# Summing squares over the chunks of d_model on VectorE before the product over partitions, and a norm issued in three parts

## The chip, the cores and the metric

The kernel runs on one core of one Trainium2 chip. The metric is device time in microseconds, the median of three runs. Five engines share the work: TensorE (PE, with its weight loads as PEld), VectorE (DVE), ScalarE (ACT), GpSimd (POOL) and SyncE (SP). Each works through its own instructions in the order in which they were issued, and waits on semaphores for the others.

## What is computed

Retention attention on 8 sequences of 576 tokens, 8 heads of 64, then a SwiGLU feed-forward network (FFN) with an RMS norm in front of it, all in float32 (the weights come as float64 and are rounded on the chip):

```python
scores = scale * np.matmul(q, k.transpose(0, 1, 3, 2))
ret = scores * Dmat                       # decay, zero above the diagonal
x = np.matmul(ret, v)                     # -> (4608 tokens, 512)
rms = np.sqrt(np.mean(x * x, axis=-1, keepdims=True) + 1e-06)
xn = x / rms * rms_g
g = xn @ w_gate                           # (512, 1536)
out = (g / (1 + np.exp(-g)) * (xn @ w_val)) @ w_out
```

## The kernel before

x is kept transposed: d_model lies on the partitions in four chunks of 128 (a chunk is a pair of heads), the tokens lie along the free axis. The FFN works on units of 384 tokens, so there are 12 units, and four of them fit on the chip.

**Attention.** One step (`attention_step`) is one key tile of 128 and one block of queries for a pair of heads: `scores` (two products `s`, L145, and their decay multiply on VectorE, `ret`, L149), then `finish`, which runs `values` (two products `av`, L165) of the step before. After the last key tile ScalarE copies `av` into the unit's `x` (L173). At the third and fifth step of a job the next job's q and k are turned on TensorE (`tp_q`, `tp_k`, L115) and copied by ScalarE (L118). Three buffers hold `s`, two are shared by `tp` and `av`.

**Norm.** When the last chunk of a unit is written, `values` returns true and `finish` calls `norm_1`: ScalarE squares the whole unit (`sq`, L185, 1536 columns), TensorE sums the squares over d_model with the squares as the weights and one column of 1/512 as the moving operand (`ms`, L188: 3 token tiles by 4 chunks, 12 products), VectorE adds epsilon (`r`, L193), GpSimd raises to -1/2 (L194), VectorE lays the result on the diagonals of three square tiles (`diag`, L197). One step later `norm_2` spreads it over the partitions with one product (`rb`, L206), and VectorE scales x by it in four instructions (L210).

**FFN.** A unit has 24 projections (`gate` and `val` in turn, L218, 4 products of 384 columns each), SiLU on ScalarE (L228) and a multiply on VectorE (`h`, L233), then 9 contract steps of 4 products of 512 columns (`out`, L241). Three PSUM buffers are shared by `gate`, `val`, `out`, `ms` and `rb`.

A product of float32 operands is two matmul instructions and two weight loads in the profile, so that the 12 products `ms` of a norm are 24 there.

**Order.** One loop (L386 to L406) issues either an attention step or an FFN step. An FFN step is taken when the FFN is behind a fixed share of the attention (`due`) and a unit is ready, else an attention step; where the next unit isn't ready, attention goes on alone. `turned` runs `norm_2` and makes the unit ready. Each pass also counts as a step for the norm: `norm_2` comes at the second pass after `norm_1`. Every second attention step rounds one chunk of the weights, six instructions on VectorE and one on ScalarE (L323 to L354), until all 36 are done.

Of the kernel before, what the change touches and what calls it, by code (L numbers as in the profile page):

```python
# [10 lines left out]
F32 = mybir.dt.float32  # L11
U32 = mybir.dt.uint32
AF = mybir.ActivationFunctionType
ALU = mybir.AluOpType
P = 128


def _decay_table(H, S, D):
    """T[p, h, c] = gamma_h ** (c - p) / sqrt(D) where c >= p, else 0: a key tile that begins at
    token t uses column q - t for query q."""  # L20
    gamma = 1.0 - 2.0 ** (-5.0 - np.arange(H, dtype=np.float64))
    rel = np.arange(S)[None, :] - np.arange(P)[:, None]
    t = np.where(rel >= 0, gamma[:, None, None] ** np.maximum(rel, 0)[None], 0.0) / np.sqrt(D)
    return np.ascontiguousarray(t.transpose(1, 0, 2)).astype(np.float32)
# [3 lines left out]
def kernel(  # L28
# [11 lines left out]
    nc = tc.nc  # L40
    B, H, S, D = q.shape
    NTOK, DM = out.shape
    DFF = moe_w_gate.shape[1]
    NHP = H // 2  # head pairs, which are also the 128-row chunks of d_model
    NF = DFF // P
    NKT = -(-S // P)  # key tiles; the last one is short
    JT = 6  # token tiles of a loaded q or k
    PT = S // JT
    U = 384  # tokens of a unit of the FFN
    NU = NTOK // U  # L50
    XBUFS = 4  # units of x on chip
    EPS = 1e-6
    assert (D, DM, NHP * P) == (64, H * D, DM) and S % JT == 0 and NTOK % U == 0

# [9 lines left out]
    ps_f = ctx.enter_context(tc.tile_pool(name="ps_f", bufs=3, space=PS))  # L64

    ident = const.tile([P, P], F32, name="ident")
    mean_w = const.tile([P, 1], F32, name="mean_w")
# [10 lines left out]
    st = [{} for _ in jobs]  # L78
    x_of = {}

# [1 line left out]

    def load(j):
        b, hp = jobs[j]
# [19 lines left out]
        st[j]["v"] = t  # L104

    def turn(j, nm):
        """q or k of a head pair with (head, d) on the partitions."""
        d = st[j]
        t = att.tile([P, S], F32, tag=nm + "T", name=f"{nm}T_{j}")
        tv = t.rearrange("p (j t) -> p j t", j=JT)  # L110
        half = JT // 2
        for n in range(2):
            tp = ps_m.tile([P, half, PT], F32, tag="m", name=f"tp_{nm}_{j}_{n}")
            for i in range(half):
                nc.tensor.transpose(  # L115
                    out=tp[:, i], in_=d[nm + "raw"][:, n * half + i], identity=ident[:PT, :PT]
                )
            nc.scalar.copy(out=tv[:, n * half : (n + 1) * half], in_=tp)  # L118
        d[nm + "T"] = t

    def blocks(b):
        """The queries of a sequence, cut where the FFN's units are."""
        cuts = [0] + [c - b * S for c in range(0, NTOK, U) if 0 < c - b * S < S] + [S]
        return list(zip(cuts[:-1], cuts[1:]))

# [6 lines left out]
        ]  # L132

    def scores(j, q0, q1, kt):
        """ret[key, query] of one key tile and one block of queries, for both heads."""
        d = st[j]
        hp = jobs[j][1]
        k0, k1 = kt * P, min(kt * P + P, S)
        lo, n = max(q0, k0), k1 - k0
        w = q1 - lo  # L140
        ret = att.tile([P, 2, U], F32, tag="ret", name=f"ret_{j}_{q0}_{kt}", bufs=3)
        ss = [ps_s.tile([P, 512], F32, tag="s", name=f"s_{j}_{q0}_{kt}_{e}") for e in range(2)]
        for e in range(2):
            r = slice(e * D, e * D + D)
            nc.tensor.matmul(  # L145
                ss[e][:n, :w], lhsT=d["kT"][r, k0:k1], rhs=d["qT"][r, lo:q1], start=True, stop=True
            )
        for e in range(2):
            nc.vector.tensor_tensor(  # L149
                out=ret[:n, e, :w], in0=ss[e][:n, :w],  # L150
                in1=decay[:n, 2 * hp + e, lo - k0 : q1 - k0], op=ALU.mult,
            )
        d["ret", q0, kt] = ret
# [19 lines left out]
            nc.scalar.copy(out=x_of[u][:, hp, c0 : c0 + q1 - q0], in_=av[:, : q1 - q0])  # L173
        return last and hp == NHP - 1 and (b * S + q1) % U == 0

# [1 line left out]

    NS = U // P

    def norm_1(u):  # L180
        """1 / rms with the tokens on the partitions, as the diagonals of square tiles."""
        x = x_of[u]
        ms = ps_f.tile([P, 512], F32, tag="f", name=f"ms_{u}")
        sq = ffn.tile([P, NHP, U], F32, tag="sq", name=f"sq_{u}", bufs=1)
        nc.scalar.activation(out=sq, in_=x, func=AF.Square)  # L185
        for s in range(NS):
            for c in range(NHP):
                nc.tensor.matmul(  # L188
                    ms[:, s : s + 1], lhsT=sq[:, c, s * P : s * P + P], rhs=mean_w,
                    start=(c == 0), stop=(c == NHP - 1),  # L190
                )
        r = ffn.tile([P, NS], F32, tag="r", name=f"r_{u}")
        nc.vector.tensor_scalar(out=r, in0=ms[:, :NS], scalar1=EPS, scalar2=None, op0=ALU.add)  # L193
        nc.gpsimd.tensor_tensor(out=r, in0=r, in1=mhalf.to_broadcast([P, NS]), op=ALU.pow)  # L194
        diag = ffn.tile([P, NS, P], F32, tag="diag", name=f"diag_{u}", bufs=1)
        for s in range(NS):
            nc.vector.tensor_scalar(  # L197
                out=diag[:, s], in0=ident, scalar1=r[:, s : s + 1], scalar2=None, op0=ALU.mult
            )
        return diag  # L200

    def norm_2(u, diag):
        """The diagonals summed over the partitions are 1 / rms in a row, on every partition."""
        x = x_of[u]
        rb = ps_f.tile([P, 512], F32, tag="f", name=f"rb_{u}")
        nc.tensor.matmul(  # L206
            rb[:, :U], lhsT=ones, rhs=diag.rearrange("p s t -> p (s t)"), start=True, stop=True
        )
        for c in range(NHP):
            nc.vector.scalar_tensor_tensor(  # L210
                out=x[:, c], in0=x[:, c], scalar=rms_g[:, c : c + 1], in1=rb[:, :U],
                op0=ALU.mult, op1=ALU.mult,
            )
# [34 lines left out]
            nc.sync.dma_start(out=out[u * U + s * P : u * U + s * P + P, :], in_=o)  # L248

    def ffn_steps(u):  # L250
        """(columns of the tensor engine, what to do)"""
        hs, ps = {}, {}
        for f in range(NF):
            yield NHP * U, lambda f=f: gate(u, f, hs)
            yield NHP * U, lambda f=f: value(u, f, hs)
        for s in range(U // P):
            for f0 in range(0, NF, 4):
                yield 4 * DM, lambda s=s, f0=f0: contract(u, s, f0, f0 + 4, hs, ps)

# [1 line left out]

    LAG = 0.17
    ready = []
    behind = []
    turning = []

    def upto(t):
        """The last unit that attention writes to, in the step of t or the one behind it."""
        j, q0 = t[:2]
        return (jobs[j][0] * S + q0) // U  # L270

    def finish():
        if behind and values(*behind.pop()):
            turning.append(norm_1(len(ready) + len(turning)))

    def turned():
        if turning:
            norm_2(len(ready), turning.pop(0))
            ready.append(len(ready))

    def attention_step(n, t):
        j = t[0]
# [8 lines left out]
                if j + 3 < len(jobs):  # L291
                    load(j + 3)

# [1 line left out]

    def columns(w, src, f):
        cut = slice(f * P, f * P + P)
# [2 lines left out]
    def rows(f):  # L300
        return w_out[:, f], lambda x: x, moe_w_out, slice(None), slice(f * P, f * P + P)

    chunks = [
        c
        for f in range(NF)
        for c in (columns(w_gate, moe_w_gate, f), columns(w_val, moe_w_val, f))
    ] + [rows(f) for f in range(NF)]
# [13 lines left out]
        raw_chunks[i] = view  # L321

    def round_chunk(i):  # L323
        """float64, as pairs of words, to the nearest float32. The mantissa is summed as
        (1.m * 2 ** 20), in one rounding; sign and exponent are put together as bits, with
        the exponent held in float32's range."""
        if i not in raw_chunks:
            return
        dst = chunks[i][0]
# [34 lines left out]
    with tc.manual_schedule():  # L364
# [17 lines left out]
        attn = [(n, t) for j in range(len(jobs)) for n, t in enumerate(tiles(j))]  # L382
        n_attn = len(attn)
        ffn_cols = sum(c for u in range(NU) for c, _ in ffn_steps(u))
        did_a, did_f, unit, steps, waited = 0, 0, 0, None, False
        while did_a < n_attn or unit < NU:  # L386
            if turning and waited:
                turned()
            waited = bool(turning)
            if steps is None and unit < len(ready):  # L390
                steps = ffn_steps(unit)
            due = did_a == n_attn or (did_a / n_attn - LAG) * ffn_cols > did_f * (1 - LAG)
            if steps is not None and (due or unit + XBUFS <= upto(attn[did_a][1])):
                got = next(steps, None)
                if got is None:
                    unit, steps = unit + 1, None
                    continue
                did_f += got[0]
                got[1]()
            elif did_a < n_attn:  # L400
                attention_step(*attn[did_a])
                did_a += 1
                if did_a > 8 and did_a % 2:
                    weights_to(n_chunks + 1)
                if did_a == n_attn:
                    finish()  # L406
# [27 lines left out]
```

## Time and profile before

| what | value |
|---|---|
| median of 3 runs | 1737.68 us (1737.16 to 1738.85) |
| span of the profiled execution | 1732.1 us |
| mean granted clock of TensorE | 0.917 |
| TensorE busy | 1609.2 us, 93% |
| VectorE busy | 387.0 us, 22% |
| ScalarE busy | 213.7 us, 12% |
| GpSimd busy | 10.9 us, 1% |

The profiled execution's own time is its span, from the first instruction to the last; the median of the runs lies 5.6 us above it, which is what lies around the instructions. A granted clock of 1.00 is 2.4 GHz and 0.50 is 1.2 GHz. Busy time of a pipelined engine doesn't say that it works at its peak, so the wait lists and the granted clock are read beside it.

### The profile page before, as it was taken

To read this page: it belongs to the slowest core of one execution; us is meant where nothing else is said; L and a number is where in the kernel's file an instruction comes from. 1 tells how busy PE (TensorE), PEld (TensorE's weight loads), DVE (VectorE), ACT (ScalarE), POOL (GpSimd) and SP (SyncE) were. 2 spreads that over 40 slices of the span, in tenths; PEclk is the share of its full clock that TensorE was granted. 3 is DMA by queue.
4 is the path that set the end of the run, shared out by engine and by line. 5 is a ranking of instruction groups with operands and counts; after the bars stand their busy time and mean duration, and the time that the engine had idled before them with its cause. 6 is when DMAs were issued, how large, how long until landed. Compare 5 with 4: busy or idle time off the path is not lost.

```text
span 1732.1 us, 14109 instructions
## 1 busy us (share of the span) xinstructions
PE 1609.2 (93%) x5784; PEld 842.0 (49%) x5784; DVE 387.0 (22%) x940; ACT 213.7 (12%) x422; POOL 10.9 (1%) x18
## 2 busy tenths in 40 slices
PE   5778976999999999999999899999999899999899
PEld 2334532554454554554554554454554554455454
DVE  2655375121111111211111211310111310410110
ACT  1112121110011110110110100110110100200000
POOL 0000000000000000000000000000000000000000
PEclk9556976999998999998999899899899899989899
DMA  6333232100100100100000101200101200100000
GB/s 180 100 88 89 60 113 80 27 14 13 33 14 20 31 17 20 47 0 20 26 21 19 41 1 28 59 0 13 27 7 32 56 1 0 46 1 6 12 0 18
DMA packets 134927, 59.89 MB, mean 35 GB/s; under 512 B 115920, under 2 KB 128208, under 8 KB 134864
## 3 DMA queue, kind: packets, MB, share of 16 engines
q1 hardware_dynamic: 119360, 37.77, 8.7%
q10 hardware_dynamic: 15504, 21.24, 3.9%
q8 instruction: 45, 0.74, 0.2%
q14 instruction: 18, 0.15, 0.0%
HBM read 49.55 MB, written 9.44 MB: 34 GB/s over the span
## 4 chain that ended last, share of the span: by engine, by line
PE 88%; DVE 6%; ACT 4%; issue 1%; DMA 1%; POOLq 0%; SPq 0%; ACTq 0%; DVEq 0%
PE gate L218 23%; PE out L241 22%; PE val L218 22%; PE s L145 8%; PE av L165 7%; PE ms L188 3%; PE tp_k L115 2%; PE tp_q L115 1%; ACT exp L338 1%; DVE exp L342 1%; ACT sq L185 1%; ACT kT L118 1%; PE rb L206 1%; DVE exp L339 1%; ACT x L173 1%
## 5 line engine op out<-in xcount | busy, mean ns | idle before, releaser
L241 PE MATMUL out<-w_out,h 128*128 128x512 f32 x864 | 402.8, 619 | 23.4 <-DVE w_out L352 23.4
L218 PE MATMUL gate<-x,w_gate 128*128 128x384 f32 x1152 | 411.9, 502 | 5.8 <-DVE x L210 5.8
L218 PE MATMUL val<-x,w_val 128*128 128x384 f32 x1152 | 397.8, 488 | 0.0
L218 PEld LDWEIGHTS gate<-x,w_gate 128*128 128x128 f32 x1152 | 221.7, 195 | 168.3 <-issue 15.9
L218 PEld LDWEIGHTS val<-x,w_val 128*128 128x128 f32 x1152 | 216.6, 190 | 151.4 <-issue 5.8
L241 PEld LDWEIGHTS out<-w_out,h 128*128 128x128 f32 x864 | 165.3, 197 | 232.6 <-issue 191.2
L149 DVE TENSOR_TENSOR ret<-s,decay 128x384 f32<-128x384 f32 (+4 forms) x480 | 160.2, 374 | 527.3 <-PE s L145 526.0
L233 DVE TENSOR_TENSOR h<-silu,val 128x384 f32<-128x384 f32 x144 | 79.8, 554 | 612.4 <-PE val L218 612.1
L145 PE MATMUL s<-qT,kT 64*128 64x384 f32 (+4 forms) x960 | 189.9, 433 | 23.5 <-DVE ret L149 23.3
L145 PEld LDWEIGHTS s<-qT,kT 64*128 64x128 f32 (+1 forms) x960 | 88.2, 198 | 146.9 <-issue 109.5
L228 ACT ACTIVATE silu<-gate 128x384 f32<-128x384 f32 x144 | 70.7, 491 | 697.7 <-PE gate L218 686.7
L165 PE MATMUL av<-ret,v 128*64 128x384 f32 (+4 forms) x960 | 156.2, 407 | 0.0
L165 PEld LDWEIGHTS av<-ret,v 128*64 128x64 f32 (+1 forms) x960 | 51.3, 146 | 74.9 <-issue 61.1
L188 PE MATMUL ms<-mean_w,sq 128*128 128x1 f32 x288 | 55.5, 325 | 26.9 <-ACT sq L185 26.9
L188 PEld LDWEIGHTS ms<-mean_w,sq 128*128 128x128 f32 x288 | 54.4, 293 | 29.1 <-ACT sq L185 29.1
L247 ACT COPY o<-out 128x512 f32<-128x512 f32 x36 | 21.1, 586 | 341.7 <-PE out L241 341.7
L115 PE MATMUL tp_k<-ident,kraw 96*128 96x96 f32 x192 | 33.5, 291 | 19.4 <-ACT kT L118 15.5
L115 PE MATMUL tp_q<-ident,qraw 96*128 96x96 f32 x192 | 32.6, 291 | 18.3 <-DMA qraw<-in_q_dram 9.7
L173 ACT COPY x<-av 128x384 f32<-128x384 f32 (+1 forms) x64 | 25.5, 399 | 177.4 <-PE av L165 153.4
L118 ACT COPY kT<-tp_k 128x288 f32<-128x288 f32 x64 | 25.5, 399 | 129.0 <-PE tp_k L115 128.9
L115 PEld LDWEIGHTS tp_k<-ident,kraw 96*128 96x128 f32 x192 | 20.5, 156 | 41.4 <-ACT kT L118 21.9
L115 PEld LDWEIGHTS tp_q<-ident,qraw 96*128 96x128 f32 x192 | 21.1, 160 | 32.1 <-issue 15.7
(33 smaller groups left out, 261.4 us busy)
## 6 DMA issues: line engine op xcount, KB each, us to landing
qraw<-in_q_dram SPq DMA_DIRECT2D x64, 144.0 KB, 2.5
kraw<-in_k_dram SPq DMA_DIRECT2D x64, 144.0 KB, 2.5
out_dram<-o SPq DMA_DIRECT2D x36, 256.0 KB, 2.1
v<-in_v_dram SPq DMA_DIRECT2D x64, 128.0 KB, 2.5
w<-in_moe_w_gate_dram ACTq DMA_DIRECT2D x12, 512.0 KB, 3.4
w<-in_moe_w_val_dram ACTq DMA_DIRECT2D x12, 512.0 KB, 3.6
w<-in_moe_w_out_dram ACTq DMA_DIRECT2D x12, 512.0 KB, 3.4
decay<-decay_table ACTq DMA_DIRECT2D x4, 576.0 KB, 6.3
```

Of the source, the lines that this page charges most:

```text
L115: nc.tensor.transpose(out=tp[:, i], in_=d[nm + "raw"][:, n * half + i], identity=ident[:PT, :PT])
L118: nc.scalar.copy(out=tv[:, n * half : (n + 1) * half], in_=tp)
L145: nc.tensor.matmul(ss[e][:n, :w], lhsT=d["kT"][r, k0:k1], rhs=d["qT"][r, lo:q1], start=True, stop=True)
L149: nc.vector.tensor_tensor(out=ret[:n, e, :w], in0=ss[e][:n, :w], in1=decay[:n, 2 * hp + e, lo - k0 : q1 - k0], op=ALU.mult,)
L165: nc.tensor.matmul(av[e * D : e * D + D, lo - q0 : q1 - q0], lhsT=d["v"][:n, e, kt], rhs=ret[:n, e, : q1 - lo], start=(kt == 0), stop=last,)
L173: nc.scalar.copy(out=x_of[u][:, hp, c0 : c0 + q1 - q0], in_=av[:, : q1 - q0])
L188: nc.tensor.matmul(ms[:, s : s + 1], lhsT=sq[:, c, s * P : s * P + P], rhs=mean_w, start=(c == 0), stop=(c == NHP - 1),)
L218: nc.tensor.matmul(ps[:, :U], lhsT=w[:, c, f * P : f * P + P], rhs=x_of[u][:, c], start=(c == 0), stop=(c == NHP - 1),)
L228: nc.scalar.activation(out=hs[f], in_=ps[:, :U], func=AF.Silu)
L233: nc.vector.tensor_tensor(out=h, in0=hs[f], in1=ps[:, :U], op=ALU.mult)
L241: nc.tensor.matmul(ps[s][:, :DM], lhsT=hs[f][:, s * P : s * P + P], rhs=w_out[:, f], start=(f == 0), stop=(f == NF - 1),)
L247: nc.scalar.copy(out=o, in_=ps[s][:, :DM])
```

## The change

`norm_1` is cut in two. The new `norm_0`, called where `norm_1` was, squares the unit on ScalarE and then adds the four chunks on VectorE, in place, in two instructions: 768 columns, then 384. `norm_1` sums what is left over the partitions, with one product a token tile (3 instead of 12), and the rest of it is as it was. `turned` is now called at every pass and counts: the third pass after `norm_0` issues `norm_1`, the third after that issues `norm_2` and makes the unit ready. Only the oldest of the units in `turning` is counted. Comments and docstrings are removed, which moves the line numbers.

```diff
-    def norm_1(u):
+    def norm_0(u):
         x = x_of[u]
-        ms = ps_f.tile([P, 512], F32, tag="f", name=f"ms_{u}")
         sq = ffn.tile([P, NHP, U], F32, tag="sq", name=f"sq_{u}", bufs=1)
         nc.scalar.activation(out=sq, in_=x, func=AF.Square)
+        n = NHP
+        while n > 1:
+            n //= 2
+            nc.vector.tensor_tensor(
+                out=sq[:, :n], in0=sq[:, :n], in1=sq[:, n : 2 * n], op=ALU.add
+            )
+        return sq
+
+    def norm_1(u, sq):
+
+        ms = ps_f.tile([P, 512], F32, tag="f", name=f"ms_{u}")
         for s in range(NS):
-            for c in range(NHP):
-                nc.tensor.matmul(
-                    ms[:, s : s + 1], lhsT=sq[:, c, s * P : s * P + P], rhs=mean_w,
-                    start=(c == 0), stop=(c == NHP - 1),
-                )
+            nc.tensor.matmul(
+                ms[:, s : s + 1], lhsT=sq[:, 0, s * P : s * P + P], rhs=mean_w,
+                start=True, stop=True,
+            )
...
     def finish():
         if behind and values(*behind.pop()):
-            turning.append(norm_1(len(ready) + len(turning)))
+            u = len(ready) + len(turning)
+            turning.append([u, 0, norm_0(u), 0])
 
     def turned():
-        if turning:
-            norm_2(len(ready), turning.pop(0))
-            ready.append(len(ready))
+
+
+        if not turning:
+            return
+        t = turning[0]
+        t[3] += 1
+        if t[3] < 3:
+            return
+        u, part, got, _ = t
+        if part == 0:
+            turning[0] = [u, 1, norm_1(u, got), 0]
+        else:
+            norm_2(u, got)
+            turning.pop(0)
+            ready.append(u)
...
-            if turning and waited:
-                turned()
-            waited = bool(turning)
+            turned()
```

On TensorE, at the norm of the seventh unit (number 6, counted from 0), the order before is this; `av_0` writes the unit's last chunk, `s_384` and `av_384` belong to the next attention steps, `tp_k` turns k:

```order
L165 MATMUL av_0_3985<-ret_0_2_3988,v_3511 64x128 x2
L188 MATMUL ms_4018<-mean_w,sq_4019 128x1 x12
L145 MATMUL s_384_1_0_4041<-qT_3873,kT_3920 128x192
L145 MATMUL s_384_1_1_4042<-qT_3873,kT_3920 128x192
L165 MATMUL av_384_4047<-ret_384_0_4008,v_3511 64x192 x2
L115 MATMUL tp_k_0_4051<-ident,kraw_3736 128x96 x3
L115 MATMUL tp_k_1_4056<-ident,kraw_3736 128x96 x3
L206 MATMUL rb_4071<-diag_4036,ones 128x384
L218 MATMUL gate_0_4077<-x_3468,w_gate 128x384 x4
```

The same place on TensorE after the change, from the same `av_0` on:

```order
L165 MATMUL av_0_3943<-ret_0_2_3946,v_3469 64x128 x2
L145 MATMUL s_384_1_0_3981<-qT_3831,kT_3878 128x192
L145 MATMUL s_384_1_1_3982<-qT_3831,kT_3878 128x192
L165 MATMUL av_384_3987<-ret_384_0_3966,v_3469 64x192 x2
L115 MATMUL tp_k_0_3991<-ident,kraw_3694 128x96 x3
L115 MATMUL tp_k_1_3996<-ident,kraw_3694 128x96 x3
L145 MATMUL s_384_2_0_4012<-qT_3831,kT_3878 128x192
L145 MATMUL s_384_2_1_4013<-qT_3831,kT_3878 128x192
L165 MATMUL av_384_3987<-ret_384_1_3980,v_3469 64x192 x2
L197 MATMUL ms_4020<-mean_w,sq_3976 128x1 x3
L145 MATMUL s_384_3_0_4032<-qT_3831,kT_3878 128x192
L145 MATMUL s_384_3_1_4033<-qT_3831,kT_3878 128x192
```

Two attention steps now stand between `av_0` and `ms`, and three more stand between `ms` and `rb`, which is followed by `gate_0` as before. The other norms are of three kinds: numbers 0, 4, 6, 7, 9 and 10 have two attention steps between, as here; 1 and 3 have one contract step and one attention step; 2, 5, 8 and 11 have projections alone.

On VectorE, the same place before; `ret` is the decay multiply of the attention steps:

```order
L149 TENSOR_TENSOR ret_384_0_4008<-s_384_0_0_4009,decay 128x192
L149 TENSOR_TENSOR ret_384_0_4008<-s_384_0_1_4010,decay 128x192
L193 TENSOR_SCALAR r_4033<-ms_4018 128x3
L197 TENSOR_SCALAR diag_4036<-ident,r_4033 128x128 x3
L149 TENSOR_TENSOR ret_384_1_4040<-s_384_1_0_4041,decay 128x192
L149 TENSOR_TENSOR ret_384_1_4040<-s_384_1_1_4042,decay 128x192
L210 SCALAR_TENSOR_TENSOR x_3468<-x_3468,rms_g,rb_4071 128x384 x4
```

And on VectorE after the change, where the two additions to `sq` are new:

```order
L149 TENSOR_TENSOR ret_384_0_3966<-s_384_0_0_3967,decay 128x192
L149 TENSOR_TENSOR ret_384_0_3966<-s_384_0_1_3968,decay 128x192
L188 TENSOR_TENSOR sq_3976<-sq_3976 128x768
L188 TENSOR_TENSOR sq_3976<-sq_3976 128x384
L149 TENSOR_TENSOR ret_384_1_3980<-s_384_1_0_3981,decay 128x192
L149 TENSOR_TENSOR ret_384_1_3980<-s_384_1_1_3982,decay 128x192
L149 TENSOR_TENSOR ret_384_2_4011<-s_384_2_0_4012,decay 128x192
L149 TENSOR_TENSOR ret_384_2_4011<-s_384_2_1_4013,decay 128x192
L202 TENSOR_SCALAR r_4024<-ms_4020 128x3
L206 TENSOR_SCALAR diag_4027<-ident,r_4024 128x128 x3
L149 TENSOR_TENSOR ret_384_3_4031<-s_384_3_0_4032,decay 128x192
```

The additions stand ahead of the `ret` of the next attention step, and `r` and `diag` ahead of the `ret` of the step that follows `ms`.

At the end of the program, on TensorE, the last norm (number 11) stood alone before: the last `av`, then `ms`, `rb` and `gate_0`:

```order
L165 MATMUL av_192_6220<-ret_192_4_6463,v_5960 64x64 x2
L188 MATMUL ms_6475<-mean_w,sq_6476 128x1 x12
L206 MATMUL rb_6497<-diag_6493,ones 128x384
L218 MATMUL gate_0_6503<-x_5991,w_gate 128x384 x4
L218 MATMUL val_0_6510<-x_5991,w_val 128x384 x4
```

After the change the FFN of unit 10 (`x_5244`) begins behind the last `av`, and the norm of unit 11 stands within it:

```order
L165 MATMUL av_192_6132<-ret_192_4_6164,v_5890 64x64 x2
L215 MATMUL rb_6180<-diag_6151,ones 128x384
L227 MATMUL gate_0_6186<-x_5244,w_gate 128x384 x4
L227 MATMUL val_0_6193<-x_5244,w_val 128x384 x4
L227 MATMUL gate_1_6200<-x_5244,w_gate 128x384 x4
L197 MATMUL ms_6207<-mean_w,sq_6176 128x1 x3
L227 MATMUL val_1_6218<-x_5244,w_val 128x384 x4
L227 MATMUL gate_2_6225<-x_5244,w_gate 128x384 x4
L227 MATMUL val_2_6232<-x_5244,w_val 128x384 x4
L215 MATMUL rb_6239<-diag_6214,ones 128x384
```

Both FFNs that are left at the end of attention now run one behind the other.

## Rows read from the trace of the kernel before

**Rows 1.** Page, part 1: busy time of each engine, share, instructions

```profile
PE 1609.2 (93%) x5784; PEld 842.0 (49%) x5784; DVE 387.0 (22%) x940; ACT 213.7 (12%) x422; POOL 10.9 (1%) x18
```

**Rows 2.** Waits of TensorE from 290 us on: total us, times, longest us

```profile
PE ms L188 <- ACT sq L185: 22.6, 11, 2.1
...
PE gate L218 <- DVE x L210: 5.8, 7, 1.1
PE rb L206 <- DVE diag L197: 2.0, 1, 2.0
```

**Rows 3.** Groups by line, `ms`: busy us, mean ns | idle before

```profile
L188 PE MATMUL ms<-mean_w,sq 128*128 128x1 f32 x288 | 55.5, 325 | 26.9 <-ACT sq L185 26.9
```

**Rows 4.** Chain that ended last, in order of time: start us, us, what

```profile
103.59 5.28 PE ms L188 x24
...
302.93 2.84 PE ms L188 x24
...
326.32 2.58 PE val L218 x8
```

**Rows 5.** Behind `ms`, units 1 to 11: length, PE, PEld, DVE, ACT, POOL, PEclk, DMA

```profile
305.77:309.60 3.83, 3.83 (x11) 1.98 (x11) 0.84 (x4) 0.80 (x2) 0.85 (x1) 0.55 0.02 4
348.17:354.40 6.23, 6.23 (x12) 3.42 (x12) 0.84 (x4) 0.49 (x1) 0.85 (x1) 0.55 0.00 0
553.33:558.60 5.27, 5.27 (x7) 2.17 (x8) 0.84 (x4) 0.00 (x0) 0.85 (x1) 0.51 0.00 0
713.53:719.00 5.47, 5.47 (x16) 2.06 (x16) 1.86 (x6) 0.80 (x2) 0.85 (x1) 0.50 0.24 54
806.19:811.20 5.01, 5.01 (x7) 2.03 (x7) 0.84 (x4) 0.00 (x0) 0.85 (x1) 0.51 0.00 0
970.99:982.10 11.11, 9.84 (x26) 5.13 (x26) 3.56 (x10) 0.80 (x2) 0.85 (x1) 0.51 0.12 27
1117.51:1122.00 4.49, 4.49 (x15) 1.93 (x16) 1.86 (x6) 0.80 (x2) 0.85 (x1) 0.53 0.00 0
1229.75:1234.70 4.95, 4.21 (x11) 1.23 (x10) 2.14 (x8) 0.00 (x0) 0.85 (x1) 0.53 0.00 0
1373.77:1385.00 11.23, 9.96 (x25) 5.14 (x26) 3.56 (x10) 0.90 (x3) 0.85 (x1) 0.52 0.12 26
1519.11:1528.00 8.89, 7.76 (x16) 3.06 (x16) 3.96 (x10) 0.00 (x0) 0.85 (x1) 0.50 0.00 1
1629.20:1637.30 8.10, 5.38 (x8) 2.65 (x9) 3.03 (x8) 0.00 (x0) 0.85 (x1) 0.51 0.01 2
sum 74.58, PE 67.46 PEld 30.81 DVE 23.33 ACT 4.58 POOL 9.36; mean PE 6.13 PEld 2.80 DVE 2.12 ACT 0.42 POOL 0.85
```

**Rows 6.** Groups by line, VectorE: shapes, count | busy us, mean ns

```profile
L339 DVE TENSOR_SCALAR exp<-exp 128x512 uint32<-128x512 f32 x36 | 15.4, 428 | 47.4 <-ACT exp L338 47.4
...
L342 DVE SCALAR_TENSOR_TENSOR exp<-w,exp 128x512 uint32<-128x512 uint32 x36 | 24.9, 692 | 1.2
...
L233 DVE TENSOR_TENSOR h<-silu,val 128x384 f32<-128x384 f32 x144 | 79.8, 554 | 612.4 <-PE val L218 612.1 <-ACT silu L228 0.3
```

**Rows 7.** Timeline at the norm of unit 6: start us, us, engine, instruction

```profile
963.67 0.48 ACT L173 COPY x<-av 128x384 f32<-128x384 f32 x1 [0.53 <-PE av L165]
964.18 1.48 ACT L185 ACTIVATE sq<-x 128x1536 f32<-128x1536 f32 x1
...
971.03 0.16 DVE L193 TENSOR_SCALAR r<-ms 128x3 f32<-128x3 f32 x1 [7.15 <-PE ms L188]
...
972.22 0.68 DVE L197 TENSOR_SCALAR diag<-ident,r 128x128 f32<-128x128 f32 x3 [1.03 <-POOL r L194]
...
972.81 0.62 DVE L149 TENSOR_TENSOR ret<-s,decay 128x192 f32<-128x192 f32 x2
```

**Rows 8.** Timeline at the first norm: TensorE behind VectorE's queue

```profile
119.00 1.01 PE L145 MATMUL s<-qT,kT 64*128 64x192 f32 x2 [2.41 <-DVE ret L149]
```

**Rows 9.** A stretch of attention alone, columns as in rows 5

```profile
940.00:962.00 22.00, 20.91 (x100) 9.67 (x100) 5.10 (x16) 3.10 (x8) 0.00 (x0) 1.00 0.24 64
```

More of the change, by code (lines that the diff above doesn't have):

```diff
@@ L384 @@
         ffn_cols = sum(c for u in range(NU) for c, _ in ffn_steps(u))
-        did_a, did_f, unit, steps, waited = 0, 0, 0, None, False
+        did_a, did_f, unit, steps = 0, 0, 0, None
         while did_a < n_attn or unit < NU:
-            if turning and waited:
-                turned()
-            waited = bool(turning)
+            turned()
             if steps is None and unit < len(ready):
```

## The prediction

> **What bounds the kernel now.** I read the busy shares first. TensorE is busy 93% of the span and VectorE 22% [rows 1], so only what shortens TensorE's own queue or its waits can pay. The wait list of TensorE came next: from 290 us on, behind the rounding of the weights, it waits for anything but transposes at three places, and all three belong to the norm. It waits 22.6 us in 11 norms for the squares, 5.8 us for the first scaled chunk of x and 2.0 us for the diagonals [rows 2]. The groups by line then show the norm's products: 288 instructions with one moving column, busy 55.5 us [rows 3]. The chain in order of time shows a norm's 24 in 2.84 us at full clock and in 5.28 us at half [rows 4]. Last comes the granted clock behind the products, and this is what a busy share hides. In each of the 11 stretches that begin where `ms` ends, the clock stands between 0.50 and 0.55 for 3.8 to 11.2 us [rows 5]. I found no low clock elsewhere after 290 us, and a stretch of attention alone runs at 1.00 with TensorE busy 20.91 of 22 us [rows 9]. So TensorE stands still or loads one-column products for some 7 us, its clock falls, and the attention and FFN work behind it pays too.
>
> **What is removed, units 1 to 11.** Four terms, each from rows:
>
> - The products. 55.5 us less the 5.28 us of the first norm leaves 50.2 us. A quarter of the instructions remains: 6 of 24, which at full clock is 2.84 / 4 = 0.71 us a norm, 7.8 us in all. Gain 42.4 us.
> - The wait for the squares, 22.6 us, goes: two steps stand ahead of `ms` now. What is late in its place is priced below.
> - The low clock. At half clock, busy work takes twice its time, so a stretch of length L at mean clock c loses (1 - c) L. Over the eleven rows that is 1.72 + 2.80 + 2.58 + 2.73 + 2.45 + 5.44 + 2.11 + 2.33 + 5.39 + 4.45 + 3.97 = 36.0 us. Idle time in them, 74.58 - 67.46 = 7.1 us, isn't lengthened by the clock, which takes off half of it, 3.6 us [rows 5]. 32.4 us are left.
> - The last norm. Its wait for the diagonals, 2.0 us, has nothing behind it to fill it before; afterwards the FFN of unit 10 does. Of the seven waits for x, 5.8 us, five stay, where `gate_0` follows `rb` directly: 5 x 0.8 = 3.9 us. Gain 2.0 + 1.9 = 3.9 us.
>
> Together 101.3 us.
>
> **The first norm.** It lies among the rounding of the weights, at half clock: 5.28 us of products [rows 4] behind 1.48 us of squares (the length of unit 6's, rows 7). Afterwards 6 instructions at half clock take 1.32 us, and the additions enter VectorE's queue, on which the rounding runs. If squares and additions stay in the chain the gain is 6.76 - 1.32 - 1.48 - 1.56 = 2.4 us; if both are hidden, 5.4 us; if VectorE's extra waits in a full queue eat it, 0. I take 2.4.
>
> **What is added.** The two additions read 768 and 384 columns, 1152 in all, from two operands on the chip. No such instruction stands in the trace. By columns, the nearest are 428 ns and 692 ns for 512, and 554 ns for 384 with an operand in PSUM [rows 6]: 0.84, 1.35 and 1.44 ns a column, so between 0.96 and 1.66 us a norm. An added instruction can't take less than nothing, so there is no gain side. I take the middle one, which has two tensor operands on the chip too: 1.56 us. VectorE has room for 12 x 1.56 = 19 us; the price is the order, not the time.
>
> The additions wait for the squares, and the `ret` of the next attention step is queued behind them; `s` needs its buffer back from `ret`, and `av` needs `ret` itself. Such a queue is seen to stop TensorE: at the first norm a product `s` waited 2.41 us for a `ret` that stood behind other work of VectorE [rows 8]. Counted from the end of the unit's last `av`: copy and squares until 2.0 us (963.67 to 965.66), additions until 3.6, the first `ret` until 3.9 [rows 7]. TensorE has two attention steps and their transposes meanwhile, some 3 us that don't need that `ret`, but `tp_k` also needs a copy by ScalarE that is queued behind the squares. I put the stop at 1.2 to 1.5 us. Behind `ms`, `r` to the end of `diag` holds VectorE's queue for 972.22 + 0.68 - 971.03 = 1.9 us [rows 7], and the `ret` of the step issued after `ms` stands behind that; TensorE has about 1 us of other work there, so it stops for another 1 us. Before, the same `diag` was hidden because one attention step's `ret` was already through. Together 2.5 us at each of the five norms between two attention steps (4, 6, 7, 9, 10): 12.5 us. Ends: 0, where the steps cover all, and 5 us a norm, 25 us. At the six other norms an FFN step, 2.58 us or longer [rows 4], stands between, needs nothing of VectorE, and covers the additions: nothing.
>
> **The clock after the change** is the cost that no row shows. At the six norms inside the FFN, TensorE no longer stands still and the products take 0.71 us; I expect 1.00 throughout. At the five others TensorE stops twice, for 1 to 1.5 us each, with the six one-column instructions between. What fell before had about 2 us of waiting and then `ms`; so one end is no fall, 0 us, and the other a fall at all five, as long as now: 2.73 + 5.44 + 2.11 + 5.39 + 4.45 = 20.1 us [rows 5]. I take three falls at the mean of 4.0 us: 12 us.
>
> The Trainium skill speaks against the change here: "TensorE: Matmul & The Clock Gate", section "A second HAM failure mode: psum-queue depth-cycling", describes a kernel whose TensorE stood idle briefly and often between groups of matmuls, so that its clock went up and down between the two levels. The rows before the change agree in part: attention alone with short gaps stays at 1.00 [rows 9], and the clock falls where a longer wait meets `ms` [rows 5]. By that rule more of the norms fall than I take; it is the second rival below.
>
> **The sum.** 101.3 + 2.4 - 12.5 - 12 = 79.2 us less. The profiled span of 1732.1 us becomes 1652.9; with the 5.6 us by which the median of the runs lies above the span, 1658.5. I say 1658 us.
>
> **Rivals.**
>
> First, the clock stays up everywhere. For it: attention alone at 1.00 [rows 9]. Against it: the stops above. 79.2 + 12 = 91.2 us less, 1646 us.
>
> Second, the clock still falls behind every norm, because any short stop around one-column products is enough, not only 2 us of waiting and 24 of them. The price is what it costs now, 32.4 us, and the remaining products at half clock, 11 x 0.71 = 7.8 us more, in place of 12: 28.2 us more, 1687 us. For it: it fell in 11 of 11 norms. Against it: three quarters of the products and, at six norms, the whole wait are gone.
>
> Third, slower than before: VectorE's queue stops TensorE for its whole chain at every one of the 12 norms, FFN steps between or not, and each stop brings a low clock as long as that of unit 6. The chain is 3.9 + 1.9 = 5.8 us [rows 7], 69 us in all instead of 12.5; the clock costs 5.44 + 0.71 = 6.2 us, 68 us in 11 norms instead of 12. That is 112 us more, 1771 us. It decides from (101.3 + 2.4) / 12 = 8.6 us of new loss a norm. Against it: `gate`, `val` and `out` wait for nothing that VectorE is late with, and only half of the norms stand between attention steps.
>
> Fourth, the additions do not come off the path because `ms` itself waits for them as it waited for the squares. With two attention steps ahead, some 4 us, against 3.6 us of copy, squares and additions, this is a few tenths at five norms and is within the range.
>
> **How the numbers follow.** Forecast (two to four falls) 0.50; no fall 0.30; a fall at every norm 0.15; slower 0.02; the rest, 0.03, is a loss between the second and the third that I can't name. The likeliest case with the ends of its stops and of the additions runs from 1648 to 1671. The range that leaves out 2 in 10 takes in the first rival with stops smaller than assumed and stops short at the second: 1638 to 1686. A measurement of this kernel can tell about 0.2%, 3.5 us. Faster by more than that 0.97, within it 0.01, slower 0.02.
>
> **What would show it.** Right: 72 `ms` instructions, some 8 to 10 us busy; no wait of `ms` for ScalarE; granted clock 1.00 through norms 1, 2, 3, 5, 8 and 11; new waits of `s` or `av` for `ret` at norms 4, 6, 7, 9 and 10, 1 to 1.5 us each; additions of about 1.0 and 0.5 us; the last norm inside the FFN of unit 10 with TensorE busy. Wrong: low clock at norms inside the FFN, waits for `ret` of 3 us or more, or a wait of `ms` for the additions as long as the one for the squares was.

## The result: 4% faster, and the profile after

The changed kernel takes 1669.5 us (median of 4 runs, 1667.4 to 1675.7) against 1738.3 us, also of 4; the ratio is 0.9602, 95% interval 0.9579 to 0.9625. 1658 us were forecast, in a range of 1638 to 1686. The profiled execution spans 1665.9 us, 66.2 us less than before.

Busy shares and granted clock on the page after, as in [rows 1]:

```profile
span 1665.9 us, 13657 instructions
...
PE 1558.4 (94%) x5568; PEld 798.7 (48%) x5568; DVE 404.0 (24%) x964; ACT 212.8 (13%) x422; POOL 10.9 (1%) x18
```

TensorE is busy 50.8 us less, with 216 matmuls fewer; VectorE is busy 17 us more. The groups by line, which answer to [rows 3], show the products and the additions:

```profile
L188 DVE TENSOR_TENSOR sq<-sq 128x768 f32<-128x768 f32 (+1 forms) x24 | 18.2, 758 | 18.8 <-ACT sq L184 18.4
...
L197 PE MATMUL ms<-mean_w,sq 128*128 128x1 f32 x72 | 11.8, 279 | 0.0
```

72 products are left and nothing is waited for in front of them. TensorE's waits from 290 us on, as in [rows 2] (total us, times, longest):

```profile
PE gate L227 <- DVE x L219: 10.8, 6, 3.4
...
PE s L145 <- DVE ret L149: 4.2, 7, 1.2
PE av L165 <- ACT qT L118: 1.0, 2, 0.5
```

The wait for the squares and the one for the diagonals are gone. The wait of `gate` for the scaled x has grown from 5.8 to 10.8 us, and `s` now waits for `ret`.

The granted clock around norms 1, 3, 4, 5, 6, 7, 8, 9, 10 and 11, in this order (length, busy times, and the clock in the third column from the right):

```profile
298.00:311.00 13.00, 12.03 (x46) 5.14 (x42) 3.19 (x9) 1.38 (x3) 0.85 (x1) 1.00 0.17 45
531.00:544.00 13.00, 12.51 (x44) 6.06 (x43) 3.65 (x10) 1.38 (x3) 0.85 (x1) 1.00 0.10 23
686.00:703.00 17.00, 13.59 (x44) 6.82 (x44) 6.35 (x16) 2.85 (x4) 0.85 (x1) 0.60 0.16 36
706.00:719.00 13.00, 13.00 (x46) 7.96 (x45) 4.14 (x10) 1.19 (x3) 0.85 (x1) 1.00 0.00 0
930.00:946.00 16.00, 14.67 (x50) 7.97 (x51) 6.34 (x20) 0.97 (x3) 0.85 (x1) 0.57 0.17 38
1081.00:1092.00 11.00, 7.61 (x18) 4.04 (x19) 4.63 (x8) 2.45 (x3) 0.00 (x0) 0.69 0.12 27
1095.00:1108.00 13.00, 13.00 (x45) 7.89 (x44) 4.14 (x10) 1.07 (x3) 0.85 (x1) 1.00 0.00 0
1319.00:1335.00 16.00, 14.67 (x50) 7.94 (x50) 5.96 (x19) 0.81 (x2) 0.85 (x1) 0.57 0.17 38
1462.00:1478.00 16.00, 13.35 (x44) 6.73 (x45) 6.49 (x17) 2.12 (x3) 0.85 (x1) 0.57 0.00 1
1482.00:1495.00 13.00, 13.00 (x45) 7.92 (x45) 4.14 (x10) 1.35 (x3) 0.85 (x1) 1.00 0.00 0
```

With FFN steps about the norm the clock stays at 1.00 throughout, at norm 2, which isn't listed, too. At all five norms between attention steps it falls. From 300 us on TensorE spends 61 us at half clock instead of 116 (the granted clock in windows of 0.5 us, each counted with 2 x (1 - clock) of its length).

Two places show what stands still there. The timeline at norm 6, where the additions hold the `ret` of the next step:

```profile
929.16 1.55 DVE L188 TENSOR_TENSOR sq<-sq 128x768 f32<-128x768 f32 x2 [1.82 <-ACT sq L184]
...
930.63 0.88 DVE L149 TENSOR_TENSOR ret<-s,decay 128x192 f32<-128x192 f32 x3
...
931.03 1.00 PE L145 MATMUL s<-qT,kT 64*128 64x192 f32 x2 [0.58 <-DVE ret L149]
...
932.80 1.44 PE L197 MATMUL ms<-mean_w,sq 128*128 128x1 f32 x6
```

VectorE stood for 1.82 us on the squares, then added for 1.55 us, and only then came to the `ret` that `s` needs. The `s` at 931.03 already runs at half clock, as does the `ms` behind it (6 in 1.44 us). And behind norm 4, where x of unit 4 waits for the squares of unit 5:

```profile
692.69 1.48 ACT L184 ACTIVATE sq<-x 128x1536 f32<-128x1536 f32 x1
...
694.20 1.55 DVE L188 TENSOR_TENSOR sq<-sq 128x768 f32<-128x768 f32 x2 [1.45 <-ACT sq L184]
695.67 2.18 DVE L219 SCALAR_TENSOR_TENSOR x<-x,rms_g,rb 128x384 f32<-128x384 f32 x4
...
696.33 5.49 PE L227 MATMUL gate<-x,w_gate 128*128 128x384 f32 x8 [2.65 <-DVE x L219]
```

The squares of unit 5 were issued before the spreading of unit 4, so its additions stand ahead of the scaling that `gate_0` of unit 4 waits for.

The start of the program comes in two forms, whatever the kernel: in one the clock rises at about 22 us and all that follows is some 5 us earlier (last section). Both kernels' profiled executions have the earlier form. The experiments are therefore also compared from the first `gate` to the end. It is the first of the two times in each row, the kernel before first:

```profile
L218 PE MATMUL gate<-x,w_gate x1152: 486/486/1009, 153.8 to 1694.4; 128*128 128x384 f32 x192
```

```profile
L227 PE MATMUL gate<-x,w_gate x1152: 486/486/1010, 146.4 to 1628.2; 128*128 128x384 f32 x192
```

7.4 us were gained ahead of the first `gate`, and 1578.3 - 1519.5 = 58.8 us behind it.

### The profile page after: what moved, and what is told of

It reads as the page before. It is cut to its first block, busy times and chain, and to the rows that moved or that the text cites. A ratio compares the mean times of both kernels' runs of the same rounds, so it can differ in the third digit from the quotient of the medians.

```text
span 1665.9 us, 13657 instructions
## 1 busy us (share of the span) xinstructions
PE 1558.4 (94%) x5568; PEld 798.7 (48%) x5568; DVE 404.0 (24%) x964; ACT 212.8 (13%) x422; POOL 10.9 (1%) x18
## 4 chain that ended last, share of the span: by engine, by line
PE 87%; DVE 7%; ACT 4%; issue 1%; DMA 1%; POOL 0%; SPq 0%; ACTq 0%; POOLq 0%
PE gate L227 23%; PE val L227 22%; PE out L250 22%; PE s L145 8%; PE av L165 7%; PE tp_k L115 2%; PE tp_q L115 1%; ACT exp L360 1%; DVE exp L364 1%; DVE exp L361 1%; DVE sq L188 1%; ACT kT L118 1%; DVE ret L149 1%; ACT sq L184 1%; DMA kraw<-in_k_dram 1%
## 5 line engine op out<-in xcount | busy, mean ns | idle before, releaser
L227 PE MATMUL gate<-x,w_gate 128*128 128x384 f32 x1152 | 409.8, 500 | 10.8 <-DVE x L219 10.8
L250 PE MATMUL out<-w_out,h 128*128 128x512 f32 x864 | 396.1, 611 | 23.4 <-DVE w_out L374 23.4
L145 PE MATMUL s<-qT,kT 64*128 64x384 f32 (+4 forms) x960 | 196.1, 432 | 29.9 <-DVE ret L149 29.8
L145 PEld LDWEIGHTS s<-qT,kT 64*128 64x128 f32 (+1 forms) x960 | 91.8, 198 | 153.7 <-issue 106.2
L118 ACT COPY qT<-tp_q 128x288 f32<-128x288 f32 x64 | 25.1, 398 | 73.6 <-PE tp_q L115 71.7
L360 ACT ACTIVATE exp<-exp,least 128x512 f32<-128x512 uint32 x36 | 26.0, 722 | 65.8 <-DVE exp L356 65.8
```

The costliest lines, as they stand in the source:

```text
L145: nc.tensor.matmul(ss[e][:n, :w], lhsT=d["kT"][r, k0:k1], rhs=d["qT"][r, lo:q1], start=True, stop=True)
L227: nc.tensor.matmul(ps[:, :U], lhsT=w[:, c, f * P : f * P + P], rhs=x_of[u][:, c], start=(c == 0), stop=(c == NHP - 1),)
L250: nc.tensor.matmul(ps[s][:, :DM], lhsT=hs[f][:, s * P : s * P + P], rhs=w_out[:, f], start=(f == 0), stop=(f == NF - 1),)
L360: nc.scalar.activation(out=e.bitcast(F32), in_=e, func=AF.Relu, bias=least)
```

## The experiments

Theory 1: what is left of the low clock comes from TensorE standing still behind VectorE's queue. Theory 2: one-column products and transposes in attention alone lower it without any stop. Span, first `gate` and half clock in the table are those of one profiled execution of each kernel.

| kernel | median us | span us | first `gate` to end | half clock from 300 us on, us |
|---|---|---|---|---|
| before | 1738.3 | 1732.1 | 1578.3 | 116 |
| changed | 1669.5 | 1665.9 | 1519.5 | 61 |
| e1, additions alone | 1713.0 | 1712.4 | 1556.3 | 82 |
| e2, three parts alone | 1695.9 | 1696.0 | 1540.0 | 82 |
| e3, additions a step later | 1652.4 | 1645.3 | 1494.6 | 20 |
| e4, even lag | 1638.3 | 1638.7 | 1486.6 | 0 |
| e5, e3 and diagonals later | 1636.4 | 1629.2 | 1480.9 | 0 |
| e6, x first alone | 1661.1 | 1665.2 | 1517.5 | 65 |
| e7, before with even lag | 1731.1 | 1729.0 | 1571.6 | 88 |
| e8, e4 and e5 | 1637.7 | 1639.0 | 1483.4 | 0 |

Ratios to the kernel before, with their intervals: e1 0.986 (0.981 to 0.991), e2 0.976 (0.971 to 0.982), e3 0.951 (0.943 to 0.960), e4 0.943 (0.938 to 0.949), e5 0.942 (0.937 to 0.947), e6 0.956 (0.951 to 0.962), e7 0.995 (0.993 to 0.997), e8 0.942 (0.939 to 0.945). The medians of e1 to e6 are of two runs, which lie up to 11.7 us apart. The intervals of e3 and e6 overlap the change's 0.958 to 0.9625, so that what these two gain over the change rests on the profiled executions.

**e1, the additions without the delay.**

```diff
-            turning.append([u, 0, norm_0(u), 0])
+            turning.append(norm_1(u, norm_0(u)))     # and turned() as before the change
```

Expected: 

> One half of the change alone: the chunks are added on VectorE and three products sum over the partitions, but the norm is issued at once as before, with the products right behind the squares and the spreading one step later. Both theories: the additions come on TensorE's path, so that it waits for copy, squares and additions, about 3.7 us a norm instead of 2.1 (17 us more in 11 norms); 18 of 24 products go, 35 to 42 us less; the clock still falls at most norms. About 1715 us, a third of the change's gain or less. If the products alone were what pays, it would come to about 1695 us.

Measured: 1713 us, as both theories said. The timeline at norm 6:

```profile
961.10 1.55 DVE L188 TENSOR_TENSOR sq<-sq 128x768 f32<-128x768 f32 x2 [1.81 <-ACT sq L184]
962.79 1.33 PE L197 MATMUL ms<-mean_w,sq 128*128 128x1 f32 x6 [3.80 <-DVE sq L188]
```

Without the delay the additions lie on TensorE's path: it waits up to 3.8 us a norm, 41.1 us in 11, and the clock falls at 11 of 11 norms although only six one-column products are left. At six of them it falls within the wait, before the first product, as at norm 5, where TensorE is busy 0.00 us on both sides of the fall:

```profile
797.03:799.00 1.97, 0.00 (x0) 0.00 (x0) 0.79 (x2) 1.87 (x2) 0.00 (x0) 1.00 0.32 74
799.10:800.80 1.70, 0.00 (x0) 0.01 (x1) 1.51 (x2) 0.00 (x0) 0.00 (x0) 0.50 0.78 238
```

So a stop alone lowers it.

**e2, the delay without the additions.**

```diff
-        (the two additions in norm_0)
-            nc.tensor.matmul(ms[:, s : s + 1], lhsT=sq[:, 0, ...], rhs=mean_w, start=True, stop=True)
+            for c in range(NHP):
+                nc.tensor.matmul(ms[:, s : s + 1], lhsT=sq[:, c, ...], rhs=mean_w, start=(c == 0), stop=(c == NHP - 1))
```

Expected: 

> The other half alone: the norm is issued in three parts as in the change, but the squares are not added and the 12 products of the kernel before remain. No addition holds VectorE's queue. Theory 1 (the clock falls where TensorE stops behind VectorE's queue): with the wait for the squares gone and nothing queued ahead of the decay multiplies, the clock stays up behind most norms; 22.6 us of waits and most of 32 us of clock are gained: 1680 to 1690 us. Theory 2 (the clock falls where one-column products stand in attention alone, or are many, whatever waits): it still falls at norms 4, 6, 7, 9 and 10 and perhaps at all; 1695 to 1712 us.

Measured: 1696 us, theory 2's side. The chain at norm 3, which has FFN steps about it and where TensorE waits 0.5 us for a copy of a turned tile ahead of the products, and the granted clock around it:

```profile
549.42 3.88 PE ms L192 x24
553.30 9.03 PE out L245 x16
```

```profile
548.00:550.50 2.50, 2.01 (x20) 1.83 (x18) 0.25 (x1) 0.80 (x2) 0.00 (x0) 1.00 0.01 3
550.50:557.50 7.00, 7.00 (x20) 4.54 (x20) 0.84 (x4) 0.00 (x0) 0.85 (x1) 0.51 0.19 43
```

The clock falls at 10 of 11 norms, at six of them within the 24 products, at four up to 1.2 us behind them. At five (1, 2, 5, 10 and 11) TensorE had not stood still for as much as 0.1 us since 8 us before the products. At norm 10, which has attention alone about it, it is busy all of the 10.10 us up to the fall:

```profile
1482.40:1490.35 7.95, 7.95 (x52) 3.53 (x53) 4.78 (x14) 2.28 (x3) 0.00 (x0) 1.00 0.01 2
1490.35:1492.50 2.15, 2.15 (x22) 2.15 (x20) 0.19 (x1) 0.00 (x0) 0.00 (x0) 1.00 0.00 0
1492.50:1502.80 10.30, 9.52 (x34) 4.95 (x34) 3.90 (x12) 1.96 (x2) 0.85 (x1) 0.50 0.00 1
```

So many one-column products lower it without any stop: theory 1 as I stated it is wrong for 24 of them. Six inside the FFN don't (the rows at 1.00 above). Neither half gains what the whole does: 1578.3 - 1556.3 = 22.0 us and 38.3 us, 60.3 together, against 58.8.

**e3, the additions a step later.**

```diff
     def norm_0(u):
-        (the two additions)
+        (squares alone; norm_add(sq) does the additions)
     def turned():
         t[3] += 1
+        if t[1] == 0 and t[3] == 2:
+            norm_add(t[2])
```

Expected: 

> The changed kernel, with the two additions issued one pass later, when the squares are done, behind the decay multiply of the next attention step, and only for the oldest unit, so that the scaling of x of the unit before is never behind the next unit's additions. TensorE's order is the changed kernel's. Theory 1 (stops behind VectorE's queue lower the clock): waits of s for ret go from 4.2 us to under 1, waits of gate for x from 10.8 to about 4, the low clock at norms 4, 6, 7, 9 and 10 goes: 1630 to 1640 us. Theory 2 (attention alone with one-column products and transposes lowers it): the waits go, the low clock stays at most of the five: 1655 to 1664 us.

Measured: 1652 us, which lies between what the two theories said and outside both. The profiled execution takes 24.9 us less than the changed kernel behind the first `gate`, with the same order on TensorE. The half-clock time falls from 61 to 20 us, at norms 4, 9 and 10. Waits from 290 us on:

```profile
PE gate L229 <- DVE x L221: 4.2, 6, 0.7
PE s L145 <- DVE ret L149: 4.2, 5, 1.0
```

The wait for x went back to 4.2 us. The wait for `ret` did not go below 1 us as expected: the 4.2 us left are those behind `diag`, as at norm 4, where the clock falls in the stop (at norms 6 and 7, with stops of 0.97 and 0.75 us, it does not):

```profile
692.32 0.47 PE L145 MATMUL s<-qT,kT 64*64 64x64 f32 x2 [0.76 <-DVE ret L149]
```

**e5, the diagonals later too** (on top of e3's edit), so that `r`, the power on GpSimd and `diag` don't hold VectorE's queue.

```diff
+        if t[1] == 1 and t[3] == 2:
+            t[2] = norm_diag(t[0], t[2])
```

Expected: 

> e3, with the diagonals issued one pass before the spreading instead of right behind the products, so that VectorE doesn't wait for GpSimd with the decay multiplies queued behind it. TensorE's order is that of the change and of e3. Theory 1 (stops behind VectorE's queue lower the clock): the waits of s for ret from 290 us on, 4.2 us in e3, go below 0.5 us, and the low clock that e3 kept, 20.5 us at three norms, goes: span from the first gate to the end 1494.6 us in e3, now 1480 to 1484 us. Theory 2 (one-column products with transposes in attention alone lower the clock without a stop): the waits go, the low clock at the three norms stays: 1489 to 1492 us.

Measured: 1480.9 us from the first `gate`, as theory 1 said. No `s` waits for `ret` from 290 us on, and the clock over the whole rest is

```profile
310.00:1628.00 1318.00, 1290.86 (x4734) 672.75 (x4732) 239.86 (x602) 155.65 (x319) 8.50 (x10) 1.00 0.09 22
```

The five norms still stand in attention alone, with the same transposes and six products in the same order. What e3 and e5 move is VectorE's queue alone, and the low clock goes with it: 61, 20, 0 us. That is theory 1, for six products. One profiled execution each is the limit of it; the other runs of e3 and e5 took 10.7 us longer, and no trace shows why.

**e6, x first alone**: the additions are late only where a norm is still under way.

```diff
     def norm_0(u):
+        if not turning:
+            norm_add(sq)
     def turned():                  # the other norms add a pass later, as in e3
```

Expected: 

> The changed kernel with one thing of e3 alone: where the norm of the unit before is still on its way (units 5, 8 and 11), the additions are issued later, so that the scaling of x of that unit goes first on VectorE; all other additions stay behind the squares at once. Waits of gate for x from 10.8 to about 4.2 us; low clock that begins only at this wait (norm 7, 6.8 us) goes, and the low clock at norms 4 and 10 ends earlier; norms 4, 6, 9 and 10 still fall by the stop behind the additions: low clock 61 to 45 or 52 us. From the first gate to the end 1519.5 us in the change, now 1506 to 1512 us: a good third of e3's 25 us. If the stop at x was all, as in e3: 1495 us.

Measured: the waits of `gate` for x go from 10.8 to 4.2 us, as expected:

```profile
PE gate L231 <- DVE x L223: 4.2, 6, 0.7
PE s L145 <- DVE ret L149: 4.1, 7, 1.2
```

But the half-clock time doesn't fall (65 us): it still falls at norms 4, 6, 7, 9 and 10 and lasts longer at 6 and 9. Only 2 us come back in the profiled execution where 7 to 13 were expected. I had taken the low clock at norm 7 for the work of the wait for x. The stop behind `diag` ahead of it is the same in both kernels, but in the changed kernel the clock holds there and falls only in the wait for x, and in e6 it falls in this stop (two products `s`, changed kernel first):

```profile
1079.31 0.33 PE L145 MATMUL s<-qT,kT 64*64 64x64 f32 x2 [0.75 <-DVE ret L149]
```

```profile
1080.89 0.47 PE L145 MATMUL s<-qT,kT 64*64 64x64 f32 x2 [0.76 <-DVE ret L149]
```

So such a stop can bring the clock down and need not. The other execution of e6 took 1655 us, 11.7 us less than the profiled one, so how much e6 gains stays open.

**e4, even lag.**

```diff
-            due = did_a == n_attn or (did_a / n_attn - LAG) * ffn_cols > did_f * (1 - LAG)
+            due = did_a == n_attn or (did_a / n_attn - LAG) * ffn_cols > did_f
```

Expected: 

> The changed kernel, with the FFN kept at an even distance behind the attention (the share 1 - LAG is left out of the rule that says when an FFN step is due), so that every norm but the first has FFN steps between squares, products and spreading, and attention never goes on alone behind the start. Both theories: no low clock from 290 us on, no wait of TensorE for ret or for x beyond 1 us: some 27 us of clock, 7 us of waits for x and 4 us for ret less, 1627 to 1640 us. If the low clock came from the norm itself, wherever it stands, it would still fall at most of the 11 norms and the time would stay above 1655 us.

Measured: 1638 us. From 290 us on TensorE waits for transposes, 2.0 us once for a rounded weight and 0.5 us in three norms for the additions, and for nothing else. Its granted clock:

```profile
310.00:1637.00 1327.00, 1306.90 (x4738) 662.83 (x4736) 233.96 (x595) 155.22 (x317) 8.49 (x10) 1.00 0.08 22
```

The norm is as in the changed kernel, additions ahead of `ret` and all; FFN steps about it are enough to cover it.

**e7, the kernel before with the even lag.** The same line, in the kernel before.

Expected: 

> The kernel before with e4's even distance between FFN and attention and nothing else. If an FFN around the norm were enough by itself, it would gain as e4 does. Both theories say no: TensorE still waits 2.1 us for the squares at each norm and loads 24 one-column products, so the clock falls at all 11 norms and 22 us of waits stay; only the longer low clocks of attention alone (11 to 17 us) become shorter: 1715 to 1735 us.

Measured: 1731 us, in the range. The wait in front of the products is all there, and the clock falls at each of these ten norms (6 of the 88 us at half clock are left over from the norm before 290 us):

```profile
PE ms L188 <- ACT sq L185: 20.7, 10, 2.1
```

So the even lag gains 33 us with the change and 7 us without it: it covers, and there must be something that can be covered.

**e8, e4 with e5's parts** (both edits above).

Expected: 

> e4 with the later additions of e3 and the later diagonals of e5. e4 has no low clock and no wait of the norm left from 290 us on, so there is nothing more to gain there: within 4 us of e4's 1638 us. If VectorE's queue still delayed something in e4 that no wait shows, it would be faster than 1630 us.

Measured: 1637.7 us in 4 runs, within 1 us of e4. The two remedies are for one loss. e4, e5 and e8 beat the changed kernel by about 2%; between them the runs tell nothing.

## Why the prediction came out as it did

The forecast was right: faster, and within the range. The span fell by 66.2 us where the sum had 79.2. By its terms:

- Products: right in kind. 11.8 us are left, 1.4 of them in the first norm, so 10.4 instead of 7.8 us, since those at norms 6, 9 and 10 ran at half clock (1.44 us a norm). 2.6 us less gain.
- Wait for the squares, 22.6 us, and for the last diagonals, 2.0 us: right, both gone. The last norm lies inside the FFN, its 6 products 0.56 us of the chain.
- Six norms inside the FFN at 1.00: right.
- Stops at the five norms: forecast 12.5 us, measured 4.2 (`s`), 1.0 (`av`) and 0.8 more at `tp_k`, 6.0 us. The two additions were sized right (1.55 us against 1.56), but TensorE had more to do in the meantime than I counted: the first stop was 0.2 to 1.2 us. Behind `diag` there was none at norms 6, 9 and 10, where TensorE already ran at half clock; in e3, at full clock there, it is 0.97, 0.97 and 0.76 us. 6.5 us more gain.
- The scaling of x: forecast 3.9 us of waits, measured 10.8. "Of the seven waits for x, 5.8 us, five stay" failed: at units 4, 7 and 10 the next unit's additions stand ahead of x on VectorE. That stood in the order of VectorE's instructions, and I looked there for `ret` alone. 6.9 us less.
- The clock: "I take three falls at the mean of 4.0 us: 12 us" is the term that was mis-sized most. It fell at five of five. What the other terms leave for it is 27 us, 5.4 a fall, and the rows bear it out: 61 us at half clock, less 8.7 us of them in which TensorE stood still, lose half of the rest, 26 us. Three falls instead of five make 8 of the 15 us that are missing. The others lie in the mean of 4.0 us, which I took from the stretches behind `ms` alone, 41 us at these five norms [rows 5]. Before, the clock was low for 65 us there, but the rest of it lay in the wait and the products, which were other terms; now `ms` comes later and most of the 61 us lies on other work. 15 us less.
- The first norm: forecast 2.4 us and at most 5.4, measured 7.4. Its wait for the squares was 4.2 us and not the 1.5 us of the squares: [rows 3] has 26.9 us in 12 norms and [rows 2] 22.6 in the 11 others. The number was in the rows, and I didn't subtract. That is 2.7 of the 5.0 us more. For the rest no experiment was made; in the changed kernel the clock stood at 1.00 from 132.0 to 138.7 us, where it was 0.50 before.

-2.6 + 6.5 - 6.9 - 15.0 + 5.0 = -13.0, and 79.2 - 13.0 = 66.2 us. The sum closes because the clock's term is what the others leave. Errors of both signs kept the total near, and that is luck.

The 5.6 us between span and median do not all lie around the instructions, as the first part of this document has it: each run whose span is known takes 1.7 or 1.8 us more than its span (1667.64 and 1665.9 us). The profiled execution before was a short one; after, the median lies 3.6 us above the span.

Of the rivals, the second (a fall at every norm) was half right, for the reason that e3 and e5 show: a stop of about 1 us in attention alone can be enough. The Trainium skill, "TensorE: Matmul & The Clock Gate", section "A second HAM failure mode: psum-queue depth-cycling", tells of a clock that goes up and down where TensorE stands idle often between groups of products. The trace agrees in part: at four of the five norms the clock fell in or up to 1.3 us behind stops of 0.6 to 1.2 us, at norm 7 in a wait of 3.4 us, and in e3 it held at two norms with stops of 0.75 and 0.97 us. The third did not come: FFN steps don't wait behind the norm's work on VectorE, as e4 shows. Nor did the fourth: `ms` waits for nothing (0.0 in its row).

## What to carry to other kernels

A wait on TensorE has two prices, its own length and the clock of the work behind it: read the granted clock behind each wait before pricing its removal. When a reduction is moved to an in-order engine, list everything that is queued behind it there, work of another unit too, and issue it only when its input is done. What can't be made short should stand where independent work surrounds it: the changed kernel with its eleven norms took 33 us more where five of them stood in attention alone than where all stood among FFN steps.

## What the runs showed of the hardware

The clock can fall while TensorE is busy without a gap: in e2 it did within 24 products of one column, at norm 10 from 1.00 to 0.50 after 10.10 us without a pause. It can also hold at 1.00 through a stop at which it falls in another execution (norm 7, in the changed kernel and in e6).

The record of the granted clock can be wrong at the start. Three turned tiles at the same place, first in the changed kernel, then in e2:

```profile
22.80 0.47 PE L115 MATMUL tp_q<-ident,qraw 96*128 96x96 f32 x3
```

```profile
22.78 0.74 PE L115 MATMUL tp_q<-ident,qraw 96*128 96x96 f32 x3
```

And the same 44 us in both, changed kernel first:

```profile
36.00:80.00 44.00, 33.47 (x120) 15.89 (x120) 25.10 (x60) 8.39 (x17) 0.00 (x0) 0.50 0.39 106
```

```profile
36.00:80.00 44.00, 33.31 (x118) 15.59 (x118) 27.02 (x62) 8.01 (x16) 0.00 (x0) 1.00 0.36 101
```

TensorE's busy time is the same, so both ran at half clock; the second is recorded as 1.00, presumably because no change of the clock had been recorded yet in that execution. It had risen at 22 us in the first, which gave it 5 us: the first squares start at 102.1 us in the changed kernel, at 107.3 in e2, and up to there both issue the same. Within a kernel the executions differ by this, so that a mean clock over the span (0.915 to 0.954 for runs of the kernel before) says little.
